# Attention and expert layer on one core: the order of every engine written out by a list scheduler inside the kernel

## The chip, the cores and the metric

The kernel runs on one core of one Trainium2 chip. The metric is the device time of one execution in microseconds. Three runs of the kernel before gave 1379.43, 1379.49 and 1369.95 us; the median is 1379.43 us. Besides those there is one profiled execution, from which every duration here is taken.

## The reference

Two stages follow each other: block-causal attention over 8 batches of 8 heads (576 positions, head size 64), and a two-layer network with a gate over the 4608 resulting tokens.

```python
scores = scale * np.matmul(q, k.transpose(0, 1, 3, 2))
scores = np.where(mask, scores, -1000000000.0)       # block_i >= block_j, blocks of 64
scores = scores - np.max(scores, axis=-1, keepdims=True)
attn = np.exp(scores)
attn = attn / (np.sum(attn, axis=-1, keepdims=True) + 1e-09)
attn_out = np.matmul(attn, v)
x = attn_out.transpose(0, 2, 1, 3).reshape(B * S, H * D)      # 4608 x 512
h = x @ w_in                                                  # 512 -> 2048
sp = np.maximum(h, 0.0) + np.log1p(np.exp(-np.abs(h)))
out = (h * erf(sp)) @ w_out                                   # 2048 -> 512
```

Products are made from two parts, a rounded high part and a low part that holds the rest, so each product of the network is three matmuls (high by high, high by low, low by high). The weights come as 64-bit numbers and are cut into those parts on the core.

## The kernel before, in words

**Attention.** The heads are numbered 0 to 63, eight to a batch. Per head, `load_qk` brings k and q (one transfer of SP's queue into the staging tile st, one of POOL's queue into one of four tiles qk, two more on SP's queue that copy inside SBUF), and POOL subtracts to make the low parts (L320, L321). `maxes` computes scores on TensorE (L332, tile s) and row maxima on VectorE (L335, tile mx); the maxima are transposed (L362), copied by ScalarE (L364) and put into the qk tile by a transfer issued from ScalarE's queue (L365). `probs` recomputes the scores transposed (L378, L379, tile t), ScalarE takes the exponentials (L383) into the tile p and rounds them (L389, ph), VectorE makes the low part (L390, pl). `pv` multiplies pairs of heads with v (L422) and with ones (L445), `scale_v` (L278) and `prep_v` (L299, L300) cut v for four heads at a time from a staging tile v that has one buffer, and `normalise` divides (L461 to L479) and stores x to DRAM as x_d (L480). A group of 256 tokens of x exists when the batch that holds its last token has gone through `normalise`, so x becomes available once in eight heads.

**The network, first part.** Of the 16 blocks of 128 hidden columns the first six are done on groups of 256 tokens: 18 groups by three units of two blocks are the 54 first-part units. A unit has 24 matmuls of 256 columns (up, L154), a gate (`gate`: ScalarE L123 once and L128 four times, VectorE L130 and L135, ScalarE L136, POOL L137) and 12 matmuls of 512 columns (down, L164); three units are followed by a store of the partial sums (L209, L210). **Second part.** The other ten blocks run on nine groups of 512 tokens, one block to a unit: 90 units of 12 up and 12 down matmuls of 512 columns. The ten weights of the second part are cut by five VectorE operations per half (L98, L99, L102, L104, L105), besides ScalarE (L101, L106) and POOL (L107, L108); so are the six of the first part, early in the attention.

**What sets the order.** Steps are Python closures. For every head `merge` interleaves the lists of steps; `moe1` is called once per head (RATE = 1) and hands out one step of a first-part unit, six steps per head after the last head (RATE2 = 6). The order in which the program is written, moved by `tc.cur_priority` for some kinds (`late`, PRIO), is the priority with which the framework's scheduler then orders every engine's queue. Each engine runs its queue in order.

**PSUM** has four pools: ps_o and ps_h with two banks each, ps_a with four during attention, and ps_o2 and ps_h2 with three and one after it.

Of the kernel before, what the change touches and what calls it, by code (L numbers as in the profile page):

```python
# [32 lines left out]

@with_exitstack
def tile_attention_moe(ctx: ExitStack, tc: tile.TileContext, qk, v, w, maskrows, sels, out):
# [8 lines left out]
    SP = 640  # L44
# [8 lines left out]
    SH = 384  # L53
    p0, p1, pars, fin = PAR

# [3 lines left out]
    wpool = ctx.enter_context(tc.tile_pool(name="wpool", bufs=F1))  # L59
    xpool = ctx.enter_context(tc.tile_pool(name="xpool", bufs=2))  # L60
    mpool = ctx.enter_context(tc.tile_pool(name="mpool", bufs=3))
    ps_o = ctx.enter_context(tc.tile_pool(name="ps_o", bufs=2, space=PSUM))
    ps_h = ctx.enter_context(tc.tile_pool(name="ps_h", bufs=2, space=PSUM))
# [21 lines left out]

    def room(pool, f):
        return [pool.tile([P, 2, DM], F32R, tag=t, name=f"{t}{f}") for t in ("whi", "wlo")]

    def load_weight(whi, wlo, stage, f):

        for s in range(2):
            nm = f"{f}_{s}"
            raw = stage[0][0].tile([P, stage[0][2]], I32, tag=stage[0][1][s], bufs=stage[0][3], name=f"raw{nm}")[:, : 2 * DM].rearrange("p (n t) -> p n t", t=2)
            nc.sync.dma_start(raw.rearrange("p n t -> p (n t)"), w[f, s].bitcast(I32))
            top, low = raw[:, :, 1], raw[:, :, 0]

            bits = stage[1][0].tile([P, stage[1][2]], I32, tag=stage[1][1], bufs=stage[1][3], name=f"bits{nm}")[:, :DM]
            nc.vector.tensor_scalar(out=bits, in0=top, scalar1=3, scalar2=0x3FFFFFF8, op0=ALU.logical_shift_left, op1=ALU.bitwise_and)  # L98
            nc.vector.scalar_tensor_tensor(out=bits, in0=top, scalar=-0x40000000, in1=bits, op0=ALU.bitwise_and, op1=ALU.bitwise_or)  # L99
            sq = stage[2][0].tile([P, stage[2][2]], F32, tag=stage[2][1], bufs=stage[2][3], name=f"sq{nm}")[:, :DM]  # L100
            nc.scalar.activation(sq, f32(top), AF.Square)  # L101
            nc.vector.scalar_tensor_tensor(out=sq, in0=sq, scalar=LEAST * LEAST, in1=f32(bits), op0=ALU.is_ge, op1=ALU.mult)  # L102

            nc.vector.tensor_scalar(out=bits, in0=sq.bitcast(I32), scalar1=-0x800000, scalar2=None, op0=ALU.bitwise_and)  # L104
            nc.vector.scalar_tensor_tensor(out=f32(bits), in0=low.bitcast(U32), scalar=2.0**-52, in1=f32(bits), op0=ALU.mult, op1=ALU.mult)  # L105
            nc.scalar.copy(whi[:, s, :], sq)  # L106
            nc.gpsimd.tensor_tensor(out=sq, in0=sq, in1=f32(whi[:, s, :]), op=ALU.subtract)  # L107
            nc.gpsimd.tensor_tensor(out=wlo[:, s, :], in0=sq, in1=f32(bits), op=ALU.add)  # L108
        return whi, wlo

    gpools = [mpool]

    def gate(h, name, gpool):

        n = h.shape[1]
        last = {}
        for k, o in enumerate(PROG):
            for i in o[1:]:
                last[i] = k
        gh, gl = (gpool.tile([P, n], F32R, tag=t, name=f"{name}_{t}") for t in ("gh", "gl"))  # L120
        regs = [mpool.tile([P, n], F32, tag="r0", name=f"{name}_r0")]
        free = [f32(gl), mpool.tile([P, n], F32, tag="r1", name=f"{name}_r1")]
        nc.scalar.activation(regs[0], h, AF.Tanh, bias=const(p1), scale=p0)  # L123
        for k, (o, pp) in enumerate(zip(PROG, pars)):
            free += [regs[i] for i in sorted(set(o[1:])) if last[i] == k]
            r = free.pop()
            if o[0] == "S":
                nc.scalar.activation(r, regs[o[1]], AF.Square, bias=const(pp[1]), scale=pp[0])  # L128
            elif o[0] == "M":
                nc.vector.scalar_tensor_tensor(out=r, in0=regs[o[1]], scalar=pp[0], in1=regs[o[2]], op0=ALU.add, op1=ALU.mult)  # L130
            else:
                nc.vector.scalar_tensor_tensor(out=r, in0=regs[o[1]], scalar=pp[0], in1=regs[o[2]], op0=ALU.mult, op1=ALU.add)
            regs.append(r)
        g = regs[-1]
        nc.vector.scalar_tensor_tensor(out=g, in0=g, scalar=fin, in1=h, op0=ALU.add, op1=ALU.mult)  # L135
        nc.scalar.copy(gh, g)  # L136
        nc.gpsimd.tensor_tensor(out=gl, in0=g, in1=f32(gh), op=ALU.subtract)  # L137
        return gh, gl

    hpools = [ps_h]  # L140
    turns = []

    def moe_unit(ws, xh, xl, o, tw, nu, u, name, first, last, spread):

        turns.append(u)
        h = hpools[len(turns) % len(hpools)].tile([P, nu, tw], F32, tag="h", name=f"{name}_h")
        parts = []

        def up(k, cs):
            whi, wlo = ws[u * nu + k]  # L150
            for cc in cs:
                sl = slice(cc * P, (cc + 1) * P)
# [25 lines left out]
    def merge(*lists):  # L178
        for step in merged(*lists):
            step()  # L180
# [36 lines left out]
    def moe1(ready, lag):  # L217
# [18 lines left out]
        if todo:  # L236
            todo.pop(0)()
# [429 lines left out]
```

## Time and profile before

| | |
|---|---|
| median of three runs | 1379.43 us |
| the profiled execution's own time | 1378.77 us |
| its span, first to last instruction | 1377.0 us |
| TensorE / ScalarE / VectorE / POOL busy | 93% / 71% / 57% / 44% |
| mean granted TensorE clock | 0.960 |

A row of the groups view names the line, engine and operation, the tile written and the tiles read, the shape and the count; then the busy time and the mean duration of one, and the engine's idle time just before these instructions with what ended it. A row of the stretches view gives, for a piece of the span, its length, then busy time and number of instructions of TensorE, its weight loads, VectorE, ScalarE and POOL, then the granted clock, the share of the transfer engines and their rate. Issuing a transfer is not counted as busy time of the engine that issues it. A matmul's row lasts longer than the distance to the next one, because matmuls overlap; TensorE's busy share therefore says that matmuls were in flight, not that they came at the highest rate.

### The profile page before, as it was taken

To read this page: it belongs to the slowest core of one execution; us is meant where nothing else is said; L and a number is where in the kernel's file an instruction comes from. 1 tells how busy PE (TensorE), PEld (TensorE's weight loads), DVE (VectorE), ACT (ScalarE), POOL (GpSimd) and SP (SyncE) were. 2 spreads that over 40 slices of the span, in tenths; PEclk is the share of its full clock that TensorE was granted. 3 is DMA by queue.
4 is the path that set the end of the run, shared out by engine and by line. 5 is a ranking of instruction groups with operands and counts; after the bars stand their busy time and mean duration, and the time that the engine had idled before them with its cause. 6 is when DMAs were issued, how large, how long until landed. Compare 5 with 4: busy or idle time off the path is not lost. (4 is left out here: it accounts for less than half of the span.)

```text
span 1377.0 us, 22100 instructions
## 1 busy us (share of the span) xinstructions
PE 1277.7 (93%) x8198; PEld 1021.0 (74%) x8198; DVE 782.0 (57%) x1237; ACT 971.7 (71%) x1781; POOL 599.3 (44%) x456
## 2 busy tenths in 40 slices
PE   2798999999999989989989998699999999999998
PEld 1455677777777768767778886578888888888887
DVE  5798977777777767767772227953233233232332
ACT  1466677678877858767777777577777777777775
POOL 3776765554655545654562225652222222222221
PEclk9898799999999989999899998899999999999999
DMA  9466757766777657675237224212113112211110
GB/s 235 123 188 162 200 147 191 190 171 190 199 180 206 172 133 195 144 196 162 104 127 245 92 92 154 77 49 74 62 61 123 61 61 85 100 62 61 62 62 31
DMA packets 89372, 179.97 MB, mean 131 GB/s; under 512 B 8540, under 2 KB 27292, under 8 KB 89264
## 3 DMA queue, kind: packets, MB, share of 16 engines
q1 hardware_dynamic: 79280, 159.41, 38.8%
q0 software_dynamic: 9344, 18.97, 6.2%
q8 instruction: 65, 1.06, 0.3%
q14 instruction: 43, 0.35, 0.1%
q10 hardware_dynamic: 640, 0.17, 0.1%
HBM read 112.29 MB, written 37.75 MB: 109 GB/s over the span
## 5 line engine op out<-in xcount | busy, mean ns | idle before, releaser
L128 ACT ACTIVATE m_r<-m_r,c 128x512 f32<-128x512 f32 x576 | 414.8, 722 | 113.4 <-DVE m_r L130 98.5
L137 POOL TENSOR_TENSOR m_gl<-m_r,m_gh 128x512 fp32r<-128x512 f32 x144 | 198.0, 1375 | 474.7 <-ACT m_gh L136 420.1
L130 DVE SCALAR_TENSOR_TENSOR m_r<-m_r,m_r 128x512 f32<-128x512 f32 x144 | 111.7, 776 | 331.2 <-ACT m_r L128 326.2
L154 PE MATMUL m_h<-xh,whi 128*128 128x256 f32 (+1 forms) x648 | 213.2, 329 | 11.6 <-DVE m_r L135 11.4
L154 PE MATMUL m_h<-xl,whi 128*128 128x256 f32 (+1 forms) x648 | 211.4, 326 | 0.0
L154 PE MATMUL m_h<-xh,wlo 128*128 128x256 f32 (+1 forms) x648 | 210.5, 325 | 0.0
L383 ACT ACTIVATE p<-t 128x288 f32<-128x288 f32 (+4 forms) x384 | 141.5, 387 | 96.7 <-PE t L379 58.8
L335 DVE TENSOR_REDUCE mx<-s 64x1 f32<-64x288 f32 (+4 forms) x384 | 170.2, 468 | 67.2 <-PE s L332 64.7
L164 PE MATMUL o<-whi,m_gh 128*128 128x512 f32 x432 | 174.0, 403 | 6.9 <-ACT ob L209 4.6
L164 PE MATMUL o<-wlo,m_gh 128*128 128x512 f32 x432 | 174.7, 404 | 0.0
L390 DVE TENSOR_TENSOR pl<-p,ph 128x832 f16<-128x832 f32 (+1 forms) x128 | 161.4, 1262 | 21.3 <-ACT ph L389 20.7
L332 PE MATMUL s<-qk 68*64 68x288 f32 (+3 forms) x384 | 132.2, 364 | 25.0 <-DVE mx L335 17.1
L164 PE MATMUL o<-whi,m_gl 128*128 128x512 f32 x432 | 152.4, 403 | 1.5 <-POOL m_gl L137 1.5
L378 PE MATMUL t<-qk 69*128 69x288 f32 (+4 forms) x384 | 134.7, 352 | 18.5 <-DMA qk<-mt 9.9
L154 PEld LDWEIGHTS m_h<-xh,whi 128*128 128x128 f32 x648 | 125.4, 193 | 34.3 <-DVE m_r L135 19.5
L320 POOL TENSOR_TENSOR qk<-st,qk 64x576 fp32r<-64x576 f32 x64 | 99.2, 1550 | 105.2 <-PE t L379 27.2
L321 POOL TENSOR_TENSOR qk<-st,qk 64x576 fp32r<-64x576 f32 x64 | 113.6, 1776 | 70.6 <-DMA qk<-qk 68.0
L135 DVE SCALAR_TENSOR_TENSOR m_r<-m_r,m_h 128x512 f32<-128x512 f32 x144 | 98.4, 683 | 79.1 <-ACT m_r L128 79.1
L154 PEld LDWEIGHTS m_h<-xl,whi 128*128 128x128 f32 x648 | 125.5, 194 | 15.2 <-issue 0.2
L154 PEld LDWEIGHTS m_h<-xh,wlo 128*128 128x128 f32 x648 | 125.4, 194 | 10.9 <-issue 1.3
L136 ACT CAST m_gh<-m_r 128x512 fp32r<-128x512 f32 x144 | 89.2, 619 | 51.6 <-DVE m_r L135 50.5
L379 PE MATMUL t<-qk 128*128 128x288 f32 (+4 forms) x384 | 123.9, 324 | 0.0
(83 smaller groups left out, 2367.0 us busy)
## 6 DMA issues: line engine op xcount, KB each, us to landing
st<-qk SPq DMA_DIRECT2D x64, 288.0 KB
qk<-qk POOLq DMA_DIRECT2D x64, 288.0 KB, 4.6
qk<-qk SPq DMA_DIRECT2D x64, 288.0 KB
x_d<-xs SPq DMA_DIRECT2D x32, 576.0 KB
raw<-w SPq DMA_DIRECT2D x32, 512.0 KB
v<-v SPq DMA_DIRECT2D x16, 640.0 KB
qk<-qk SPq DMA_DIRECT2D x64, 144.0 KB
xh<-x_d SPq DMA_DIRECT2D x18, 512.0 KB
```

The lines of the kernel that those rows point to most:

```text
L128: nc.scalar.activation(r, regs[o[1]], AF.Square, bias=const(pp[1]), scale=pp[0])
L130: nc.vector.scalar_tensor_tensor(out=r, in0=regs[o[1]], scalar=pp[0], in1=regs[o[2]], op0=ALU.add, op1=ALU.mult)
L137: nc.gpsimd.tensor_tensor(out=gl, in0=g, in1=f32(gh), op=ALU.subtract)
L154: nc.tensor.matmul(h[:, k, :], lhsT=a[:, 0, sl], rhs=x[:, cc, :], start=cc == 0 and i == 0, stop=cc == NCC - 1 and i == 2)
L164: nc.tensor.matmul(o[c], lhsT=a[:, sl], rhs=b_[:, 1, :], start=first and k == 0 and not lo and b_ is whi, stop=last and k == nu - 1 and lo)
L321: nc.gpsimd.tensor_tensor(out=t[D:, 1, :], in0=st[D:, :], in1=f32(t[D:, 1, :]), op=ALU.subtract)
L332: nc.tensor.matmul(dst[:r, :w_], lhsT=qh[:K, i * P : i * P + r], rhs=kh[:K, k0 : k0 + w_], start=True, stop=True)
L335: nc.vector.tensor_reduce(out=mx[:r, col : col + 1], in_=src, axis=AX.X, op=ALU.max, negate=True)
L378: nc.tensor.matmul(s[:kk, :w_], lhsT=kh[:K, ks], rhs=qh[:K, q0 : q0 + w_], start=True, stop=False)
L379: nc.tensor.matmul(s[:kk, :w_], lhsT=klh[:, ks], rhs=qhl[:, q0 : q0 + w_], start=False, stop=True)
L383: nc.scalar.activation(p32s[part][:kk, c : c + w_ - skip], s[:kk, skip:w_], AF.Exp, scale=SCALE)
L390: nc.vector.tensor_tensor(out=pl, in0=p, in1=ph, op=ALU.subtract)
```

## The change

The same operations with the same operands are no longer emitted as they are written. Each is recorded as a task with an engine, a duration in ns, a delay after it, the tiles it reads and writes and a priority (`plan.add`); `Plan.order` then runs a list schedule over all of them, and they are traced in the order of the start times that it found, under `tc.manual_schedule()`, so that this order is every engine's queue. Tile buffers are claimed in the plan too: a task that first uses a tile can't start before the plan has a free buffer.

The priority is the number of the head at which a step is written, plus its place within that head. `pv` steps are moved ahead by 0.7 (PV), the operations of a gate by 3 (GATE). The 49 units that need no later pools have the priority max(n + 1, 10 + 1.19 x index) where n is the head at which their x is known; a lower number goes first, and a ready task of any number goes when nothing ahead of it is ready. The pools of the second part (ps_o2, ps_h2, gpool, wpool2, bpool) open when all tasks of the attention era have run in the plan (`over`). Warm-up matmuls are 80 instead of 110. `sums` is one task instead of being cut by the merge.

```diff
+    HOP = 200.0
+    SPARE = 500.0
+    SWITCH = 90.0
...
+    def add(self, eng, ns, fn, r=(), w=(), lag=0.0, mode="f", off=0.0):
+        t = Task(len(self.tasks), eng, ns, lag, fn, self.prio + off, mode, self.era)
...
+                for o in t.outs:
+                    hop = 0.0 if o.eng == t.eng and not t.lag else self.HOP + (self.SPARE if o.eng == "PE" else 0.0)
+                    o.ready = max(o.ready, now + hop)
...
+            while pending and pending[0][0] <= now:
+                _, _, t = heapq.heappop(pending)
+                insort(ready.setdefault(t.eng, []), (t.prio, t.seq, t))
...
+        return sorted(self.tasks, key=lambda t: (t.at, t.seq))
...
+    GATE = -3.0
...
+                add("ACT", 722, lambda r=r, a=a, pp=pp: nc.scalar.activation(r[0](), a[0](), AF.Square, bias=const(pp[1]), scale=pp[0]), r=[a[1]], w=[r[1]])
...
+            add("ACT", 60, lambda: nc.scalar.dma_start(f32(qks[n % NB][D + 4 : D + 5, 3 * S :]).rearrange("o (i p) -> o i p", p=P), f32(mt())),
+                r=[mt], w=Q(n, "m"), lag=2500.0)
...
+        while units1 and units1[0][0] in known and len(units1) > TAIL:
+            at = max(n + BEHIND, 9 + BEHIND + (NT // T * NU - len(units1)) * spread)
+            if at > n + 8 and n < N + 3:
+                break
+            unit1(at, False)
...
+    over = Task(len(plan.tasks), "X", 0, 0.0, None, 0.0, "f", 0)
+    over.deps = {t for t in plan.tasks if t.era == 1}
...
+    with tc.manual_schedule():
+        for t in plan.order():
+            if not opened and any(b.late for b in t.bufs):
+                opened = True
+                era.close()
...
+            if t.fn:
+                t.fn()
```

**VectorE, from its first instruction.** Before (vm, vs, vsb belong to v; bits, sq and raw to the first weight; a number after an underscore is head, batch or weight):

```order
L278 TENSOR_REDUCE vm0_0_153<-v32_0_0_151 128x1
L526 CAST id16_209<-ident_77 128x128
L98 TENSOR_SCALAR bits0_0_329<-raw0_0_327 128x512
L283 TENSOR_REDUCE vs0_0_157<-vt0_0_155 1x1
L99 SCALAR_TENSOR_TENSOR bits0_0_329<-raw0_0_327,bits0_0_329 128x512
L284 TENSOR_SCALAR vs0_0_157<-vs0_0_157 1x1
L285 RECIPROCAL vs0_0_157<-vs0_0_157 1x1
L98 TENSOR_SCALAR bits0_1_342<-raw0_1_340 128x512
```

Now:

```order
L388 CAST id16_130<-ident_77 128x128
L471 TENSOR_REDUCE mx0_126<-s01_0_157 128x1 x2
L471 TENSOR_REDUCE mx0_126<-s2_0_162 128x1
L411 TENSOR_REDUCE vm0_0_185<-v32_0_0_141 128x1
L471 TENSOR_REDUCE mx0_126<-s4_0_0_164 64x1
L471 TENSOR_REDUCE mx0_126<-s4_0_1_167 64x1
L497 TENSOR_TENSOR mx0_126<-mx0_126 64x1
L471 TENSOR_REDUCE mx1_127<-s01_1_169 128x1 x2
```

The row maxima of head 0 stand first; before, 23 other operations (v and the first weights) stand ahead of them.

**ScalarE at head 21.** p32 is the tile p, t20 and t21 are the scores of heads 20 and 21, m1_1_2 is group 1, unit 2 of the first part. Before:

```order
L383 ACTIVATE p32_1_118<-t1_20_128_2885 128x448
L383 ACTIVATE p32_1_118<-t2_20_256_2927 128x320
L383 ACTIVATE p32_0_117<-t0_21_0_2943 128x288
L389 CAST ph1_20_2931<-p32_1_118 128x768
L136 CAST m1_1_1_gh_6900<-m1_1_1_r1_6903 128x512
L123 ACTIVATE m1_1_2_r0_8122<-m1_1_2_h_7162,c1_88 128x512
L425 ACTIVATE usb9_2822<-u4_1_1_2947,vsb2_0_2247 128x320
L383 ACTIVATE p32_0_117<-t0_21_288_2959 128x288
L128 ACTIVATE m1_1_2_r0_8122<-m1_1_2_r0_8122,c2_90 128x512
```

Now:

```order
L304 ACTIVATE m1_3_0_r0_3339<-m1_3_0_h_3288,c1_88 128x512
L310 ACTIVATE m1_3_0_r0_3339<-m1_3_0_r0_3339,c2_90 128x512
L310 ACTIVATE m1_3_0_r1_3346<-m1_3_0_r0_3339,c3_92 128x512
L319 CAST m1_2_2_gh_3350<-m1_2_2_r1_3299 128x512
L310 ACTIVATE m1_3_0_r1_3346<-m1_3_0_r1_3346,c4_94 128x512
L527 ACTIVATE p32_1_118<-t1_20_128_3322 128x448
L527 ACTIVATE p32_1_118<-t2_20_256_3327 128x320
L535 CAST ph1_20_3375<-p32_1_118 128x768
L310 ACTIVATE m1_3_0_r1_3346<-m1_3_0_r1_3346,c5_96 128x512
L527 ACTIVATE p32_0_117<-t0_21_0_3341 128x288
```

Before, a gate's operations stand one at a time between those of the heads all through the attention; now gates stand in runs. TensorE's queue shows the same in numbers: before, first-part matmuls stand between the scores of every two heads from head 12 on, and 28 of the 54 units have begun when the scores of head 63 start; now six units (once nine) stand together at heads 12 to 16, 20 to 24, 28 to 31 and so on, none in between, and 45 have begun by then.

**TensorE at the end of the attention** (t63 are head 63's scores, u its product with v, o1_8_1 the output of group 8). Before:

```order
L378 MATMUL t3_63_320_8055<-qk3_101 128x256
L379 MATMUL t3_63_320_8055<-qk3_101 128x256
L164 MATMUL o1_8_1_9332<-whi3_738,m1_8_1_gl_9420 128x512
L378 MATMUL t4_63_320_8066<-qk3_101 64x256
L379 MATMUL t4_63_320_8066<-qk3_101 64x256
L378 MATMUL t1_63_128_8074<-qk3_101 128x448
```

Now:

```order
L520 MATMUL t3_63_320_10238<-qk3_110 128x256
L521 MATMUL t3_63_320_10238<-qk3_110 128x256
L520 MATMUL t4_63_320_10246<-qk3_110 64x256
L521 MATMUL t4_63_320_10246<-qk3_110 64x256
L520 MATMUL t1_63_128_10250<-qk3_110 128x448
L521 MATMUL t1_63_128_10250<-qk3_110 128x448
```

Group 8 of 18 was being worked on; now groups up to 14 are finished, and the next first-part matmul after these rows is that of group 15, whose x holds tokens of the last batch, after 158 other rows. Nine units are left instead of 26. In the second part the down matmuls of a unit stood five units behind its up matmuls; now one or two.

More of the change, by code (lines that the diff above doesn't have):

```diff
@@ L1 @@
+import heapq
+from bisect import insort
 from contextlib import ExitStack
@@ L92, in load_weight @@
             nm = f"{f}_{s}"
[L93 to L98, printed above, removed]
@@ L105, in load_weight @@
[L105 to L115, printed above, removed]
+            braw = buf(stage[0][0], [P, stage[0][2]], I32, stage[0][1][s], f"raw{nm}", stage[0][3])
```

1008 lines of the change are left out of this document (588 added, 420 removed).

## The prediction

> **What bounds the kernel now.** I read the page first. It looks bound by TensorE, and I do not believe it for the whole span:
>
> ```profile
> PE 1277.7 (93%) x8198; PEld 1021.0 (74%) x8198; DVE 782.0 (57%) x1237; ACT 971.7 (71%) x1781; POOL 599.3 (44%) x456
> ```
>
> So next the stretches view, in four pieces: up to head 12, heads 12 to 63, the rest of the first part, the second part (times of TensorE, weight loads, VectorE, ScalarE, POOL), and below it five pieces of 50 us.
>
> ```profile
> 0.00:169.00 169.00, 124.86 (x850) 80.70 (x850) 135.70 (x222) 83.05 (x179) 107.42 (x98) 0.90 0.68 181
> 169.00:683.00 514.00, 486.41 (x4131) 386.44 (x4130) 378.05 (x655) 383.13 (x829) 280.97 (x205) 0.95 0.65 173
> 683.00:885.00 202.00, 185.41 (x1112) 156.56 (x1112) 106.64 (x133) 148.43 (x240) 82.84 (x57) 0.96 0.40 137
> 885.00:1377.00 492.00, 481.07 (x2111) 397.32 (x2109) 161.65 (x230) 357.06 (x535) 128.10 (x97) 0.99 0.20 67
> ...
> 50.00:100.00 50.00, 46.87 (x336) 29.10 (x334) 43.86 (x72) 30.51 (x69) 32.59 (x25) 0.96 0.67 176
> 100.00:150.00 50.00, 44.42 (x332) 28.89 (x331) 41.75 (x76) 29.49 (x68) 35.42 (x23) 0.79 0.61 170
> 300.00:350.00 50.00, 48.24 (x431) 38.35 (x431) 39.30 (x74) 40.85 (x91) 27.39 (x23) 1.00 0.69 192
> 850.00:900.00 50.00, 36.71 (x120) 27.67 (x121) 49.59 (x54) 31.18 (x53) 32.61 (x22) 0.80 0.32 106
> 1000.00:1050.00 50.00, 50.00 (x222) 41.44 (x221) 15.39 (x23) 37.02 (x55) 11.64 (x9) 1.00 0.26 85
> ```
>
> The second part is bound by TensorE: 222 matmuls of 512 columns in 50 us are 0.225 us each, and 90 units of 24 are 486.5 of its 492 us. No order shortens that. Heads 12 to 63 are different. At 0.225/512 = 0.44 ns a column a head has 5696 columns of scores (2.5 us), half a pair's 4800 columns against v (the two heads of a pair start together, 0.13 to 0.14 us for 320 columns in the rows below: 1.0 us) and, I estimate from what is left, 0.8 us of sums and transposes, 4.3 us in all. 26 units of 5.5 us come to that, 51 x 4.3 + 143 = 362 of 514 us: "busy" says 486 because each row outlasts the distance to the next.
>
> ```profile
> 481.51 0.30 PE L422 MATMUL u<-ph,vl 128*64 128x320 f16 x2
> 481.65 0.30 PE L422 MATMUL u<-pl,vh 128*64 128x320 f16 x2
> 481.78 0.30 PE L422 MATMUL u<-ph,vh 128*64 128x320 f16 x2
> ```
>
> What fills the heads is ScalarE, of whose time issuing the maxima's transfer (0.70 us a head) isn't in the busy column: 383.1 + 50 x 0.70 = 418 of 514 us, 81%, and 44.4 of 50 (89%) in the best piece. VectorE has 74%. Neither is full; they wait for each other in order. One such stall, of VectorE and then ScalarE:
>
> ```profile
> L365 ACTq DMA_DIRECT2D qk<-mt x64: 693/700/1264, 38.5 to 675.0; - x64
> ...
> 483.74 1.49 DVE L278 TENSOR_REDUCE vm<-v 128x1 f32<-128x1280 f32 x1 [5.47 <-DMA v<-v]
> ...
> 487.28 0.41 ACT L383 ACTIVATE p<-t 128x288 f32<-128x288 f32 x1 [6.40 <-DVE pl L390]
> ...
> DVE vm L278 <- DMA v<-v: 29.4, 8, 10.0
> ```
>
> A reduction of v stood at the head of VectorE's queue before its data had landed; pl behind it waited, and ScalarE waited for pl. Eight such waits are 29 us.
>
> **The change part by part.** It removes 30 warm-up matmuls, which only fill time in which TensorE waits for the first data, and adds nothing; the rest is order. I cost the warm-ups, the sums in one piece and the claims on PSUM at nothing (were the warm-ups in the way, 30 x 0.22 = 7 us). The transfers stay the same in number; a head's own (288 + 288 + 288 + 144 + 160 + 288 KB by the page) come to 1.46 MB, 200 GB/s at 7.25 us a head, and at 0.65 busy for 173 GB/s the transfer engines carry that at three quarters, so SP's queue is not the next to be late. *(a) Start.* The scores of head 0 are there at 14.8, their maxima begin at 27.8 because v and weights stand ahead on VectorE:
>
> ```profile
> 14.84 1.99 PE L332 MATMUL s<-qk 68*128 68x256 f32 x6
> ...
> 27.77 4.72 DVE L335 TENSOR_REDUCE mx<-s 128x1 f32<-128x128 f32 x12
> ```
>
> Now the maxima stand first. But VectorE must still cut six weights and serve twelve heads before head 12, and 135.7 of 169 us are already work: of the 33 us idle some 10 precede the first data. I take 10 us (0 to 20).
>
> *(b) Heads 12 to 63.* What a unit costs ScalarE and VectorE comes from these groups of the same 514 us:
>
> ```profile
> L128 ACT ACTIVATE m_r<-m_r,c 128x512 f32<-128x512 f32 x105 | 75.5, 720 | 2.3 <-DVE m_r L130 2.2
> L123 ACT ACTIVATE m_r<-m_h,c 128x512 f32<-128x512 f32 x26 | 17.8, 685 | 0.0
> L136 ACT CAST m_gh<-m_r 128x512 fp32r<-128x512 f32 x26 | 16.1, 619 | 0.9 <-DVE m_r L135 0.8
> L209 ACT COPY ob<-o 128x512 f32<-128x512 f32 x16 | 9.3, 579 | 1.0 <-PE o L164 1.0
> ...
> L130 DVE SCALAR_TENSOR_TENSOR m_r<-m_r,m_r 128x512 f32<-128x512 f32 x27 | 23.0, 851 | 0.3 <-ACT m_r L128 0.3
> L135 DVE SCALAR_TENSOR_TENSOR m_r<-m_r,m_h 128x512 f32<-128x512 f32 x26 | 17.5, 672 | 0.5 <-ACT m_r L128 0.5
> ```
>
> ScalarE (75.5 + 17.8 + 16.1 + 9.3)/26 = 4.56 us, VectorE 1.56 us. Without the units (118.7 and 40.5 us) and the few weight operations at the end of the stretch (about 5 and 12 us) a head costs ScalarE (418 - 118.7 - 5)/51 = 5.8 us and VectorE (378 - 40.5 - 12)/51 = 6.4 us. Now 45 units lie in this stretch, about 6.75 to every eight heads, and they lie together. I cost a period of eight heads in two pieces. The burst: four heads with 6.75 units, TensorE 4 x 4.3 + 6.75 x 5.5 = 54 us, ScalarE 4 x 5.8 + 6.75 x 4.56 = 54 us; at the 89% that ScalarE reaches in its best piece, 60.5 us. Four heads alone: VectorE bounds, 6.4 us at the 88% that it had from 50 to 100 us (43.86 of 50), 7.25 us, together 29 us. Period 89.5 us against 8 x 514/51 = 80.6 us now; 6.4 periods are 573 us, 59 more than 514. Bounds: ScalarE's whole work is 8 x 5.8 + 6.75 x 4.56 = 77 us, so 80 us is the least; the burst one after the other with the heads (the last rival) is 110 us. I stand nearer the lower end since 89% and 88% are rows of engines working beside each other, as they must here. The planned durations are near the rows (722 ns for L128, 720 here); the worst, the maxima's transfer at 60 ns against 700, is inside my 5.8 us, but the plan doesn't see it, which is why I don't go below 89%.
>
> *(c) After the last head.* Before, 26 units take 683 to about 886, which is 1377 - 486.5 and some 4 us for the end. Now nine are left, 9 x 5.5 = 50 us, but all nine need the last batch, and nothing covers it: from the last scores to the last store of x,
>
> ```profile
> L378 PE MATMUL t<-qk x384: 278/332/802, 40.4 to 683.4; 69*128 69x288 f32 x63, 69*128 69x256 f32 x63, 69*128 69x448 f32 x63, 69*128 69x320 f32 x2
> ...
> L480 SPq DMA_DIRECT2D x_d<-xs x32: 359/377/383, 101.3 to 699.3; - x32
> ...
> L187 SPq DMA_DIRECT2D xh<-x_d x27: 359/386/1165, 148.6 to 1250.3; - x27
> ...
> L154 PE MATMUL m_h<-xh,whi x648: 274/283/793, 155.9 to 1358.1; 128*128 128x256 f32 x108, 128*128 128x512 f32 x54
> ```
>
> 16 us, then the store (I estimate 5 us, from POOL's 4.6 us landings on the page) and from the first load to the first matmul 7 us: 28 us in which TensorE has only the end of the attention. Its cover, units of earlier groups, is gone. So 203 us become 78.
>
> *(d) The ten weights.* One costs VectorE twice the sum of these means, 8.5 us:
>
> ```profile
> L99 DVE SCALAR_TENSOR_TENSOR bits<-raw,bits 128x512 int32<-128x512 int32 x32 | 34.0, 1062 | 0.4
> L102 DVE SCALAR_TENSOR_TENSOR sq<-sq,bits 128x512 f32<-128x512 f32 x32 | 29.6, 925 | 1.7 <-ACT sq L101 0.6 <-DVE bits L99 0.5
> L105 DVE SCALAR_TENSOR_TENSOR bits<-raw,bits 128x512 f32<-128x512 uint32 x32 | 29.0, 907 | 0.4
> L98 DVE TENSOR_SCALAR bits<-raw 128x512 int32<-128x512 int32 x32 | 26.0, 812 | 7.9 <-POOL wlo L108 5.0 <-DMA raw<-w 2.9
> L104 DVE TENSOR_SCALAR bits<-sq 128x512 int32<-128x512 int32 x32 | 17.6, 550 | 0.3
> ```
>
> They stopped TensorE before: 13 us at 850 to 900, with VectorE at 49.59 of 50. Now 85 us of weights and 19 gates of 1.5 us stand in 78 us and the 54 us of the first group, 114 of 132: VectorE just suffices, and I charge 8 us (0 to 20).
>
> *(e) Second part.* Down matmuls follow their gate more closely. In the trace a gate takes from 1000.51 (first operation) to 1008.85 (its low part done):
>
> ```profile
> 1000.51 0.67 ACT L123 ACTIVATE m_r<-m_h,c 128x512 f32<-128x512 f32 x1
> ...
> 1006.81 0.62 ACT L136 CAST m_gh<-m_r 128x512 fp32r<-128x512 f32 x1 [0.30 <-DVE m_r L135]
> ...
> 1007.56 1.29 POOL L137 TENSOR_TENSOR m_gl<-m_r,m_gh 128x512 fp32r<-128x512 f32 x1 [4.13 <-ACT m_gh L136]
> ```
>
> 8.3 us, or 6.9 for the high part that goes first. In the new queue three groups of twelve and a bit stand between, 39 matmuls of 0.225 us, 8.8 us. It fits barely; I charge 7 us for 90 units (0 to 45, half a us each, were the gates late).
>
> *Sum*, in the profiled execution's own time (1378.8 us with 1.8 us around the span; the median is 1379.4): 683 - 10 + 59 + 78 + 8 + 491 + 7 + 2 = **1318 us**, 61 us less.
>
> **The rivals.** *The period shrinks to 80 us* because waits like v's all go: VectorE reached 99% at 850 to 900. Against it, there it worked on weights alone. 6.4 x 9.5 = 61 us less, and (e) at nothing: 1250 us.
>
> *The clock falls in the heads without units.* At 100 to 150 us, where the heads run alone, the row has clock 0.79 and 332 matmuls, at 300 to 350 clock 1.00 and 431. Heads alone then cost TensorE 8.6 us at half the clock instead of 7.25 us: 1.35 x 4 x 6.4 = 35 us more, 1353 us. For it speaks the row; against it that TensorE would then be full and the clock rises again. [...]
>
> *The gain is eaten*: ScalarE keeps its 81% (period 77/0.81 = 95 us) and the gates of (e) are late by a third of a us each, 30 us instead of 7: 1318 + 6.4 x 5.5 + 23 = 1376 us, no change.
>
> *Slower: bursts run instead of heads.* Gates have their priority moved ahead by 3, so on ScalarE they go before the exponentials of the heads; each unit's matmuls then take 5.5 us while heads stand, 6.75 x 5.5/0.9 = 41 us, and eight heads alone cost 8.6 us each (6.4 us at the 74% that VectorE has now, since p has one buffer and makes the two wait as in the 6.40 us row): 41 + 69 = 110 us. That is 1318 + 6.4 x 20.5 = 1449 us. It decides from a period of 99 us on. For it speaks the order with four gate operations in a row; against it that exponentials of the running heads stand between them.
>
> **How the numbers follow.** Chances: my sum 0.48, the short period 0.14, the clock 0.10, eaten 0.13, slower 0.15. A measurement here tells from no change what differs by about 1%, 14 us (1365.6 to 1393.2). The first three lie below 1366 but for a part of their spread: faster 0.70; within 1% 0.15; slower 0.15. The range goes from the short period, 1250, up to the eaten gain and a little of the slow case, 1390.
>
> **What would show it.** Right: the last scores at about 732 us, first-part matmuls in seven bursts, ScalarE in the stretch from head 12 at 85 to 90% with issues, a TensorE gap of 20 to 30 us behind the last head, the second part in 492 to 500 us. The waits of vm for v mostly gone. Wrong in (b): last scores beyond 790 us, heads standing still during bursts. Wrong in (c): the gap over 40 us. Wrong in (e): TensorE under 95% after the first group, released by gates. If the end of attention comes before 690 us, I took the shares of ScalarE and VectorE too low.

## The result, and the profile after

The changed kernel takes 1526.61 us (median of four runs, 1524.83 to 1530.26) against 1379.46 us for the kernel before on the same chip: ratio 1.1096, 95% interval 1.1035 to 1.1156. It is 147 us slower; the forecast was 61 us faster. The profiled execution took 1524.83 us, its span 1522.9 us. The page, then the stretches view in the four pieces of the prediction (up to head 12, heads 12 to 63, the rest of the first part, the second part), cut where they now end; a head is placed by the start of its 448-column score matmul:

```profile
PE 1365.3 (90%) x8168; PEld 1083.9 (71%) x8168; DVE 791.7 (52%) x1237; ACT 984.4 (65%) x1781; POOL 580.0 (38%) x456
```
```profile
0.00:203.00 203.00, 143.06 (x931) 97.36 (x932) 143.95 (x227) 92.47 (x190) 112.48 (x102) 0.74 0.61 156
203.00:900.00 697.00, 654.65 (x4655) 517.89 (x4653) 390.54 (x684) 472.56 (x940) 283.77 (x219) 0.83 0.50 137
900.00:1034.00 134.00, 94.14 (x526) 79.03 (x524) 89.73 (x104) 80.31 (x134) 61.01 (x42) 0.83 0.42 148
1034.00:1523.00 489.00, 473.41 (x2064) 389.67 (x2062) 167.50 (x224) 339.02 (x518) 122.74 (x94) 0.99 0.20 67
```

The second row holds the loss: 697 us where before had 514. It holds 42 units now instead of 26 (by their up matmuls), yet VectorE does nearly the same work in it (390.5 against 378.1 us), and ScalarE's busy share falls from 75% to 68%: the stretch is not fuller, it waits. The third row is 134 us instead of 202, and 86 was forecast. The second part has hardly changed (489 us, before 492).

Where TensorE's up matmuls of the network lie, in 40 equal slices of the span, first before, then after (lines: up is L330 after the change, down L349, scores L520 and L521, scores for the maxima L467, exponentials L527, a gate's ScalarE L304 and L310, its VectorE L314 and L318, maxima L471, a weight's first VectorE operation L277):

```profile
busy tenths in 40 slices 0000656577665637656499999999999999999996
```
```profile
busy tenths in 40 slices 0000690890970990980940929977999999999997
```

Before, every slice has some of them from the fifth on; after, they come in blocks with empty slices between, as the order had shown. TensorE inside one block, from the timeline:

```profile
396.60 0.44 PE L521 MATMUL t<-qk 128*128 128x288 f32 x1
396.84 0.41 PE L330 MATMUL m_h<-xh,whi 128*128 128x256 f32 x1
...
404.53 0.28 PE L330 MATMUL m_h<-xh,wlo 128*128 128x256 f32 x1
404.74 0.30 PE L569 MATMUL u<-ph,vh 128*64 128x256 f16 x2
...
420.38 0.28 PE L330 MATMUL m_h<-xh,wlo 128*128 128x256 f32 x1
420.50 0.28 PE L520 MATMUL t<-qk 69*128 69x256 f32 x1
```

Between the scores at 396.60 and the next at 420.50 lie 24 us: 48 ups (two units), products with v and sums, one score tile for the maxima, twelve ups, the 24 downs of two units, 36 more ups. TensorE is dense (busy 23.5 of the 24 us), but the running head gets none of its scores t, and the engines behind it stand still, as the waits of ScalarE and VectorE in the same 24 us say, and the waits view of the whole span, after and then before:

```profile
401.98 0.69 ACT L304 ACTIVATE m_r<-m_h,c 128x512 f32<-128x512 f32 x1 [4.46 <-PE m_h L330]
...
420.94 0.69 DVE L314 SCALAR_TENSOR_TENSOR m_r<-m_r,m_r 128x512 f32<-128x512 f32 x1 [10.29 <-ACT m_r L310]
```
```profile
DVE m_r L314 <- ACT m_r L310: 269.9, 106, 11.3
DVE mx L471 <- PE s L467: 171.6, 117, 14.3
...
ACT m_r L304 <- PE m_h L330: 128.1, 84, 7.5
```
```profile
DVE m_r L130 <- ACT m_r L128: 326.2, 106, 4.0
DVE mx L335 <- PE s L332: 64.7, 102, 2.1
...
ACT m_r L123 <- PE m_h L154: 3.7, 5, 1.9
```

The columns are us in total, number of waits, the longest. VectorE's wait inside the gates was larger in total before, so it is not the loss. What has grown are the waits for TensorE: VectorE waits 171.6 us for score tiles to take maxima from instead of 64.7, ScalarE 128.1 us for a unit's ups instead of 3.7.

### The profile page after: what moved, and what is told of

Its sections match the earlier page's. It is cut to its first block, busy times and chain, and to the rows that moved or that the text cites. A ratio compares the mean times of both kernels' runs of the same rounds, so it can differ in the third digit from the quotient of the medians.

```text
span 1522.9 us, 21901 instructions
## 1 busy us (share of the span) xinstructions
PE 1365.3 (90%) x8168; PEld 1083.9 (71%) x8168; DVE 791.7 (52%) x1237; ACT 984.4 (65%) x1781; POOL 580.0 (38%) x456
## 4 chain that ended last, share of the span: by engine, by line
PE 51%; ACT 8%; DVE 6%; DMA 3%; issue 2%; SPq 1%; POOL 0%; DVEq 0%; ACTq 0%; POOLq 0%
PE o L349 20%; PE m_h L330 20%; ACT m_r L310 3%; PE u L569 3%; PE s L467 2%; PE t L520 2%; PE t L521 1%; DMA qk<-mt 1%; ACT p L527 1%; DMA raw<-w 1%; PE us L594 1%; PE rt L612 1%; PE rb L630 1%; DVE m_r L314 1%; ACT m_r L304 1%
## 5 line engine op out<-in xcount | busy, mean ns | idle before, releaser
L310 ACT ACTIVATE m_r<-m_r,c 128x512 f32<-128x512 f32 x576 | 406.6, 720 | 72.3 <-DVE m_r L314 56.1
L314 DVE SCALAR_TENSOR_TENSOR m_r<-m_r,m_r 128x512 f32<-128x512 f32 x144 | 126.0, 875 | 286.9 <-ACT m_r L310 269.9
L471 DVE TENSOR_REDUCE mx<-s 64x1 f32<-64x288 f32 (+4 forms) x384 | 170.3, 468 | 173.1 <-PE s L467 171.6
L330 PE MATMUL m_h<-xh,whi 128*128 128x256 f32 (+1 forms) x648 | 218.6, 337 | 35.5 <-DVE m_r L318 25.2
L527 ACT ACTIVATE p<-t 128x288 f32<-128x288 f32 (+4 forms) x384 | 140.7, 387 | 131.2 <-PE t L521 107.5
L330 PE MATMUL m_h<-xl,whi 128*128 128x256 f32 (+1 forms) x648 | 215.4, 332 | 2.0 <-DMA xl<-x_d 2.0
L330 PE MATMUL m_h<-xh,wlo 128*128 128x256 f32 (+1 forms) x648 | 215.0, 332 | 0.0
L520 PE MATMUL t<-qk 69*128 69x288 f32 (+4 forms) x384 | 153.7, 401 | 38.7 <-DVE mx L471 18.4
L349 PE MATMUL o<-whi,m_gh 128*128 128x512 f32 x432 | 176.6, 409 | 10.7 <-ACT m_gh L319 10.6
L304 ACT ACTIVATE m_r<-m_h,c 128x512 f32<-128x512 f32 x144 | 98.6, 684 | 129.1 <-PE m_h L330 128.1
L467 PE MATMUL s<-qk 68*128 68x256 f32 (+3 forms) x384 | 145.5, 417 | 33.9 <-DMA qk<-qk 21.1
L349 PE MATMUL o<-wlo,m_gh 128*128 128x512 f32 x432 | 172.7, 400 | 0.0
L330 PEld LDWEIGHTS m_h<-xh,whi 128*128 128x128 f32 x648 | 132.3, 204 | 50.4 <-DVE m_r L318 27.2
L536 DVE TENSOR_TENSOR pl<-p,ph 128x832 f16<-128x832 f32 (+1 forms) x128 | 147.2, 1153 | 15.4 <-ACT ph L535 14.8
L318 DVE SCALAR_TENSOR_TENSOR m_r<-m_r,m_h 128x512 f32<-128x512 f32 x144 | 98.5, 684 | 106.6 <-ACT m_r L310 106.3
L455 POOL TENSOR_TENSOR qk<-st,qk 64x576 fp32r<-64x576 f32 x64 | 102.5, 1602 | 112.2 <-PE t L521 30.1
L330 PEld LDWEIGHTS m_h<-xl,whi 128*128 128x128 f32 x648 | 132.2, 204 | 11.9 <-DMA xl<-x_d 2.3
L330 PEld LDWEIGHTS m_h<-xh,wlo 128*128 128x128 f32 x648 | 131.8, 203 | 8.8
L521 PE MATMUL t<-qk 128*128 128x288 f32 (+4 forms) x384 | 137.2, 359 | 0.0
L520 PEld LDWEIGHTS t<-qk 69*128 69x128 f32 (+1 forms) x384 | 83.5, 217 | 73.4 <-DVE mx L471 26.6
L456 POOL TENSOR_TENSOR qk<-st,qk 64x576 fp32r<-64x576 f32 x64 | 101.2, 1582 | 68.9 <-DMA qk<-qk 66.3
```

The costliest lines, as they stand in the source:

```text
L304: add("ACT", 690, lambda: nc.scalar.activation(br[0](), h(), AF.Tanh, bias=const(p1), scale=p0), r=kh, w=[br[0]])
L310: add("ACT", 722, lambda r=r, a=a, pp=pp: nc.scalar.activation(r[0](), a[0](), AF.Square, bias=const(pp[1]), scale=pp[0]), r=[a[1]], w=[r[1]])
L314: add("DVE", 890, lambda r=r, a=a, c=c, pp=pp, ops=ops: nc.vector.scalar_tensor_tensor(out=r[0](), in0=a[0](), scalar=pp[0], in1=c[0](), o ...
L330: nc.tensor.matmul(bh()[:, k, :], lhsT=a(0)[:, cc * P : (cc + 1) * P], rhs=x()[:, cc, :], start=cc == 0 and i == 0, stop=cc == NCC - 1 and ...
L349: nc.tensor.matmul(o[c](), lhsT=a()[:, sl], rhs=b_(1), start=first and k == 0 and not lo and b_ is whi, stop=last and k == nu - 1 and lo)
L467: add("PE", mmns(w_), lambda: nc.tensor.matmul(s()[:r, c0 : c0 + w_], lhsT=qh[:K, i * P : i * P + r], rhs=kh[:K, k0 : k0 + w_], start=True ...
```

## The experiments

All runs are of the whole computation. Unless an interval is given a time is one run, beside a run of the kernel before at 1377 to 1381 us. Ten runs of one of these kernels lie between 1375.76 and 1386.06 us, so single runs less than about 1% apart tell no difference. "The stretch" is that from head 12 to head 63; units are counted by their up matmuls.

**Units spread over the heads, still ahead of them.**

```diff
+    for at, ups in held.items():          # ups: the unit's up matmuls
+        if int(at) + 3 < N:
+            for t in ups:
+                t.deps.add(anchor[int(at) + 3])   # scores of the third head after its number
```

> The changed kernel, but in the plan the first matmuls of a first-part unit may not start before the scores of the third head after its priority number, so that units stand one to a head and not six together (42 instead of 45 begun by the last head). Theory A, the heads that stand alone let the TensorE clock fall to half and are then bound by TensorE: clock above 0.92 from head 12 to 63 (0.83 in the changed kernel), that stretch 560 to 610 us instead of 697, time 1400 to 1450. Theory B, the planned order itself stalls the engines because its durations and waits are not those of the chip: stretch within 30 us of 697, time 1490 to 1550.

Measured: 1556.96 us, worse than the changed kernel.

```profile
185.00:925.00 740.00, 656.30 (x4694) 520.08 (x4690) 397.35 (x688) 465.25 (x938) 275.46 (x221) 0.85 0.47 130
```

Neither theory has its numbers. The clock rose to 0.85 only, so this run can't judge theory A, and the stretch is 43 us longer, where B allowed 30. What it shows is that spacing the units does not help as long as each one, once it starts, goes ahead of the heads.

**The clock.** One more 512-column matmul ahead of each score tile, in the heads without units:

```diff
             def go():
+                if n < 12 or n % 8 < 4:
+                    nc.tensor.matmul(s(), lhsT=ident16, rhs=..., start=True, stop=True)
                 nc.tensor.matmul(s()[:kk, :w_], lhsT=kh[:K, ks], ...
```

> The changed kernel in its own order, with one more matmul of 512 columns, whose result is overwritten, ahead of each score tile of the heads up to 11 and of the first four of every later eight: 6 x 0.22 us a head of added TensorE work, some 50 us in all. Theory A: the clock in the stretches without units goes from 0.61 to 0.75 up to 0.9 or more, four heads alone take about 32 instead of 40 us, time 1440 to 1480 in spite of the added work. Theory B: clock or not, the heads keep their pace or get slower by the added work, time 1520 to 1580.

Measured: 1512.71 us.

```profile
202.00:886.00 684.00, 628.61 (x4799) 492.43 (x4797) 391.36 (x684) 472.71 (x941) 280.61 (x219) 0.94 0.51 140
```

The clock is back at 0.94 and the stretch is 13 us shorter. Four heads alone went from 40.6 to 37.1 us (means over the six such groups), the four with units from 68.4 to 69.7. Theory A has its clock and not its time: raising the clock gains 14 us of 147, hardly more than single runs can tell. That is a net figure, with the filler's own work in it; the clock's whole price was not measured.

**Heads alone under the order of before.** The units of the kernel before handed out only after the last head, without and with ten warm-up matmuls a head:

```diff
-            if not xs1:
+            if n < 11:                            # warm-ups; n < N in the second run
...
-            lists.append((late("moe", [lambda: moe1(ready, LAG)] * k), 0, 1))
+            lists.append((late("moe", [lambda: moe1(ready if n >= N else 0, LAG)] * k), 0, 1))
```

> The kernel before with its scheduler, but no first-part unit before the last head (all 54 after it), so that heads 12 to 63 stand alone under the old order. Theory A: the clock falls there too, mean below 0.75, and a head takes 9.5 us or more although ScalarE and VectorE have less to do than with units (10.1 us a head with 26 units). Theory B: clock above 0.9 and 7 to 8 us a head, since nothing but the list schedule is at fault.

> The same as the one before with ten warm-up matmuls of 512 columns at every head and not only the first eleven, 2.2 us of TensorE work more per head that nothing needs. Theory A: clock 0.9 or more, and the heads get faster by 1 us or more each (about 8 to 8.5 us) with more work. Theory B: heads slower or the same as without the fillers.

Measured: 1389.79 and 1485.72 us. The first is no test: the framework's scheduler put 27.7 units back into the stretch (before has 26.1). In the second 3.8 are left there, and the heads take 473.5/51 = 9.3 us each at clock 0.96, with the filler and the 3.8 units in them. The 7.25 us of the prediction is not reached there either, but the run doesn't say what the heads alone would take.

**Units behind the heads: one number.**

```diff
-            unit1(at, False)
+            unit1(at + 200, False)
```

> One number changed: the 49 units that need no later pools get their priority plus 200, so that every head's step goes ahead of every unit and a unit only takes what the heads leave free. Theory C (the unit's number is lower than the number of the head that runs when its x arrives, about 3 heads late, and gates another 3 lower, so whole units go ahead of the heads' scores on TensorE and ScalarE and are done in series with the heads): units spread over the heads, the stretch from head 12 to head 63 falls from 697 to 520-570 us, the granted clock in it rises from 0.83 to over 0.93, and the time is 1360-1420. Rival D (the units are ready only in bursts because x is finished once in eight heads, and a list order can't spread them whatever their number): the stretch stays at 660-700 and the time at 1490-1530. Rival E (the heads' own chain is what is slow in this order, with or without units): the stretch 600-660, 1440-1490.

Measured: 1409.42 us, 117 us less than the changed kernel.

```profile
191.00:719.00 528.00, 508.48 (x4372) 412.95 (x4371) 379.38 (x660) 425.30 (x880) 274.37 (x207) 0.97 0.62 172
```
```profile
busy tenths in 40 slices 0000086896779869659489999569999999999997
```
```profile
398.49 0.28 PE L330 MATMUL m_h<-xh,wlo 128*128 128x256 f32 x1
398.61 0.37 PE L520 MATMUL t<-qk 69*128 69x448 f32 x1
...
399.17 0.31 PE L521 MATMUL t<-qk 128*128 128x320 f32 x1
399.32 0.28 PE L330 MATMUL m_h<-xh,whi 128*128 128x256 f32 x1
```

The stretch is 528 us, ScalarE is at 81%, the clock at 0.97. The empty slices between the blocks are gone, and on TensorE two tiles of scores stand between two groups of ups. Over the whole span VectorE's wait for score tiles falls from 171.6 to 99.1 us, ScalarE's for a unit's ups from 128.1 to 75.0. Theory C is shown: nothing but the units' numbers was changed, and with numbers above those of the heads the list order spreads the units by itself. Rivals D and E fall. The clock's recovery (0.83 to 0.97) is part of the 117 us.

**The gates' number.**

```diff
-    GATE = -3.0
+    GATE = 0.0
```

> The changed kernel with the gates at their unit's own number instead of 3 lower; the units' own numbers stay. My losing case in the prediction blamed this shift for the bursts. If it is what puts units ahead of heads: the stretch from head 12 to head 63 falls by over 60 us from 697 and the time below 1465. Theory C (the unit's own number is lower than that of the head that runs, gates or not): stretch 670-710 us, bursts stay, 1505-1545.

Measured: 1534.53 us, the stretch 690 us, as theory C had it. That the gates were moved ahead is not the cause.

**Units recorded after the heads.**

```diff
-        while units1 and units1[0][0] in known and len(units1) > TAIL:
+        while n >= N + 3 and units1 and units1[0][0] in known and len(units1) > TAIL:
```

> The units are recorded after all heads instead of between them, so their numbers are all above those of the heads, and the buffers that heads and units share are claimed by the heads first. Under theory C this does the same for the heads as the number plus 200: the stretch from head 12 to head 63 520-570 us, the time 1340-1420; against the other kernel it tells whether the place in the record matters as well as the number (C: within 2%). Rivals D and E: as there, 1440-1530.

Measured: 1386.91 us, 1.6% below the kernel with the number alone, within the 2% of theory C. The stretch holds 38.5 units in 549 us (35.0 in 529 there), and the last head is followed by the second part's first unit after 102 us instead of 143.

**What a head costs without units.** Recorded after the heads, held until head 63's last scores, the clock kept up (0.97 and 0.95 in the rows) by the extra matmul in every head; then the same with all eight PSUM banks for the heads:

```diff
+    for t in held:
+        t.deps.add(anchor[N - 1])
...
-        k = len(turn) % 8 if slot < 8 else 0     # only in the second of the two
+        k = len(turn) % 8
```

> Every first-part unit waits for the last scores of head 63, so the heads run alone; a 512-column matmul ahead of each score tile keeps the clock up (1.3 us of TensorE a head). All work is done, in another order. This measures a head without units in the new order: the prediction had 7.25 us (VectorE at 88%). Theory P (four PSUM banks set the pace of heads alone): 9.0-9.6 us a head, stretch 460-490 us, VectorE at 65-75% in it; the prediction's own: 7.0-7.6 us, 360-390. After the last head all 54 units and the weights: time 1430-1500.

> As the kernel before it, and the heads may use all eight PSUM banks (every second, third and fifth of eight tiles in the banks that the units would use) through the whole attention instead of up to head 8 alone. Theory P (the banks set the pace): 7.0-7.9 us a head, stretch 355-405 us, VectorE over 80% in it, time 80-110 us shorter than the kernel with four. Rival (the one buffer of each half of p, or the maxima's way through ScalarE and a transfer, sets it; or the clock): 8.7-9.6 us a head, no difference over 2%.

Measured: 1478.22 and 1460.24 us; their stretches:

```profile
192.00:630.00 438.00, 403.95 (x3435) 269.46 (x3433) 321.11 (x591) 293.58 (x648) 213.19 (x174) 0.97 0.63 168
```
```profile
185.00:602.00 417.00, 387.64 (x3464) 274.52 (x3463) 331.19 (x589) 287.58 (x645) 222.36 (x171) 0.95 0.70 179
```

A head alone is 438/51 = 8.6 us, VectorE at 73%; with eight banks 8.2 us, at 79%. Neither the prediction's 7.0 to 7.6 us nor theory P's 9.0 to 9.6 was met with four banks, and with eight theory P expected 7.0 to 7.9: four banks cost 5%, not the 1.35 us between 8.6 and 7.25. What holds the heads back with eight banks stays open; the largest waits left there are ScalarE's for scores and POOL's for a free qk tile.

**The start.** All on the kernel with units recorded after the heads, whose head 12 is at 189.5 us (before: 168.7): more warm-ups; the first two weights ahead of the maxima again; the weights written at heads 2, 3, 5, 6, 8, 9 (with the second staging tile, below).

```diff
-    WARM = 10                       # rec_warm; and for n < 11 instead of 8
+    WARM = 25
...
+    plan.prio = -1.5                # rec_early
+    for _ in range(2):
+        next_w1()
...
-    W1 = [1, 2, 3, 4, 7, 8]         # late
+    W1 = [2, 3, 5, 6, 8, 9]
```

> The kernel with the units recorded after the heads (1386.9 us, head 12 at 189.5 us, clock 0.70 up to head 11) with 275 warm-up matmuls at the lowest priority among heads 0 to 10 instead of 80 among heads 0 to 7. If the low clock is what makes the first twelve heads 20 us later than before: clock over 0.9 there, head 12 at 165-175 us, time 1362-1375. If VectorE's work is what sets them (144 us of it up to head 12, little of it in the first 30 us): clock up, head 12 at 184-192, time 1380-1392.

> The same kernel (1386.9 us) with the first two weights of the first part ahead of head 0's row maxima on VectorE, as they stood before the change. If the step that puts the maxima first is what costs the start (VectorE's time in the first 50 us is lost and the weights come back later between heads): head 0 back at 45-50 us, head 12 at 170-180 instead of 189.5, time 1367-1380. If VectorE's place for the weights doesn't matter: head 12 at 186-194, 1383-1392.

> The kernel with the second staging tile (1376.3 us, head 12 at 187.5 us) with the six weights of the first part written at heads 2, 3, 5, 6, 8, 9 instead of 1, 2, 3, 4, 7, 8. If the start is long because weight operations stand in runs ahead of the heads' maxima on VectorE, which then stands idle once the weights are done (25 of 40 us from 160 on): head 12 at 172-182, time 1362-1372. If the sum of VectorE's work with its waits sets it whatever the order: head 12 at 185-191, 1372-1382.

Measured: head 12 at 188.3, 193.5 and 193.2 us; times 1379.86, 1388.17 and 1391.79 us. From 40 to 120 us, with 80 and with 275 warm-ups:

```profile
40.00:120.00 80.00, 54.58 (x382) 35.83 (x380) 70.10 (x108) 40.19 (x85) 52.08 (x36) 0.68 0.58 154
```
```profile
40.00:120.00 80.00, 77.20 (x565) 45.35 (x563) 70.99 (x108) 40.13 (x87) 52.65 (x35) 1.00 0.58 154
```

The clock goes from 0.68 to 1.00 there, and head 12 comes 1 us earlier. From 120 to 160 us it is 0.67 in that run too, so it clears the clock for the heads up to 7 alone (119 us against 120). The second run had head 0 later than expected (55 us) and head 12 where VectorE's place for the weights doesn't matter; the third missed both of its ranges. In two executions of the kernel with the second staging tile head 12 was at 187.5 and 194.1 us, so none of the three moved it by more than it moves by itself. None explains the late start; it stays open.

**The ten weights.** The second half of each early weight staged in the tile of xs; then all of this together, the first two of the six late weights staged in tiles of the second part's x and six weights instead of five asked for ahead of the second part besides:

```diff
-        load_weight(w2[-1], (("a", ("v32", "v32"), 4 * 5 * D, 1), ...
+        load_weight(w2[-1], (("a", ("v32", "xs"), 4 * 5 * D, 1), ...
...
-    AHEAD = 5                                                            # combo alone
+    AHEAD = 6
...
-            load_weight(w2[-1], (("x", ("xh", "xl"), 2 * DM, 2), ...        # combo alone
+            load_weight(w2[-1], (("b", ...) if len(w2) < 7 else ("x", ...), ...
```

> The same kernel (1386.9 us) with the second half of each of the four early weights of the second part staged in the tile of xs, not in the one buffer of v32. Theory T (the early weights go one after the other through one buffer, about 11 us a half, and the last of them opens the second part's pools): the four are done 20-40 us earlier (the first of the later six starts at 800-820 instead of 838), the first ten units of the second part take 70-80 us instead of 93, time 1360-1377. If the four weights that must wait for the first part's buffers decide it: 88-95 us, 1380-1390.

> Everything that a run has spoken for or left undecided: units recorded after the heads, second staging tile, weights written later, 275 warm-ups, and of the six late weights the first two staged in the tiles of the second part's x instead of the first part's, which the last groups still hold. If the late weights start too late because of that staging: the first of them under 815 us, the first ten units of the second part at 70-82 us, time 1345-1365. If VectorE's own work on them (about 5 us a half) sets it: 88-95 us, 1365-1380.

> The kernel with units recorded after the heads and the second staging tile again, timed against the kernel before. By its one run (1376.3) no difference: 1370-1388, ratio 0.995-1.006. Theory C in full, with the place of the units in the order as the main cause of the loss, holds if it stays over 130 us below the changed kernel.

Measured: 1376.3 us in the first run and 1380.43 us (median of ten) in the repeat, ratio to before 1.0006, interval 0.998 to 1.0032; all together 1378.42 us, ratio 0.9989, interval 0.9958 to 1.002. The early weights begin their last half at 786 instead of 810 us, the late ones start at 827 instead of 838 (817 with all together), and the second part's first ten units take 89 us instead of 93 (82 with all together). Theory T is right about the early weights, which end 24 us sooner, and wrong about what that brings: the late ones start 11 us sooner and the first ten units save 4. All together reach the 82 us and not the time that was expected with it. No version beats the kernel before; with the units' place mended the two orders are equal within 0.5%. Of the 146 us that came back, 117 came with the number (1526.61 to 1409.42), 22.5 with the place in the record (1386.91), and 6.5 with the staging tile (1380.43), the last too little for single runs to tell.

## Why the prediction was wrong, step by step

The forecast put the last scores at 732 us; they came at 900. The 207 us between 1318 and 1525 are 44 at the start, 124 in heads 12 to 63, 48 after the last head, and -9 in the second part.

**(b) Heads 12 to 63, wrong: both pieces of the period.** The six periods after head 15 have a mean of 109 us, where I had 89.5: the four heads with units 68.4 us (62.9 to 83.4) instead of 60.5, the four alone 40.6 us (35.5 to 42.9) instead of 29. Times 6.4 that is 51 + 74 = 125 for the 124 us missed. The burst failed at the step "at the 89% that ScalarE reaches in its best piece": that row came from units lying between the operations of heads. Here they were ahead of them, and 6.5 units added (68.4 - 4 x 8.6)/6.5 = 5.2 us each, nearly the 5.5 us of TensorE that a unit holds; put behind the heads, 35 units add (528.6 - 438.6)/35 = 2.6 us each. The four heads alone failed at "VectorE bounds, 6.4 us at the 88%": VectorE's 88% was that of a piece in which it cut weights too, and heads alone give it 73%, 8.6 us. The filler took 3.5 us off four of them (40.6 to 37.1), which is what the low clock (0.83 in the stretch, 0.94 with the filler) costs them, net of the filler's own work; of the 6.2 us above 4 x 8.6 = 34.4 the other 2.7 stay open. The sign that the prediction named for this, last scores beyond 790 us and heads standing still during bursts, is what came.

**The slower rival, right in size, wrong in cause.** It had 41 + 69 = 110 us a period, with eight heads at 8.6 us each; 109 and 8.6 were measured. That the sums agree is in part luck: the units added 34 us, not 41, and 6 us lie in the four heads alone, which took 40.6 us in that order. I blamed the gates' -3. With it undone the time does not fall; the unit's own number decides. I had the order before me, with its six units in a row and none between, and the argument against the rival ("exponentials of the running heads stand between them") looked at ScalarE's queue alone. On TensorE's queue there were no scores between the ups to make exponentials from.

**The clock rival, partly right:** 0.60 to 0.64 from 50 to 150 us, 0.83 in the stretch, 0.50 from 258 to 292 us (last row below); raising it again gained 14 us net, where the rival had 35.

**(a) Start, wrong in sign.** The maxima of head 0 do begin 12 us sooner (16.0 instead of 27.8 us, its 448-column scores at 34.6 instead of 49.5), and head 11 is 18 us later (174.8 against 156.6); the first block of units makes head 12 another 16 us late. The step that failed is that what head 0 wins, head 12 wins too. By head 4 it is gone (89 us, before 86). VectorE's place for the weights is not the reason by the second run of the start; up to head 11 VectorE is busy 133.4 of 174.8 us, before 123.7 of 156.6. Why it takes longer is the open point above.

**(c) The exposed chain, right.** 28 us were forecast between the last scores and the first matmul of the last batch, 22 measured:

```profile
922.53 0.58 PE L330 MATMUL m_h<-xh,whi 128*128 128x256 f32 x1 [10.27 <-DMA xh<-x_d]
```

The nine units behind it took 63 us instead of 50 (922 to 985).

**(d) The ten weights, mis-sized.** I spread 85 us of VectorE evenly over the 132 us after the last head. The first four weights begin before the last head and pass half by half through the one buffer of v; their loads are issued at

```profile
883.96 0.33 SPq L275 DMA_DIRECT2D raw<-w  x1
896.04 0.35 SPq L275 DMA_DIRECT2D raw<-w  x1
...
942.00 0.36 SPq L275 DMA_DIRECT2D raw<-w  x1
```

and the other six start only at 973.8: their pools open when the last of the first four is done (its last POOL operation ends at 953.9), and their first load is issued at 962.7. They and the gates hold VectorE at 69.25 of 86 us while the second part's first ten units take 86 us; their matmuls are 54 us, so 32 are lost where I charged 8. In 21.2 of them, six times, TensorE waits for the gate's operation L318, which stands among those of the weights on VectorE:

```profile
985.00:1071.00 86.00, 64.54 (x244) 50.01 (x242) 69.25 (x70) 51.99 (x84) 48.80 (x32) 0.88 0.19 64
```
```profile
PE m_h L330 <- DVE m_r L318: 21.2, 6, 6.5
```

Before, the same ten units took 62 us; the six weights began 28 us ahead of them there, under first-part units. The price of 8.5 us a weight was low as well: it is the mean over all 32 halves, and the twelve late ones cost VectorE 9.8 us a weight, before and after.

**(e) Second part, right with a smaller price.** The down matmuls find their gates done; TensorE has no hole:

```profile
1100.00:1150.00 50.00, 50.00 (x223) 41.40 (x222) 15.54 (x23) 35.69 (x54) 11.65 (x9) 1.00 0.25 85
```

From the eleventh unit to the end 451.5 us against 452.1 before; the 7 us charged were not needed. **The waits for v** were to be mostly gone: vm waits 22.7 us, six times, instead of 29.4, so most of them stayed. And the count was right: 45 units had begun by head 63, though 42 of them in the stretch, where the prediction put all 45. Doing more units under the heads was worth nothing, since they took the heads' place.

## What to carry to other kernels

A list scheduler obeys the number; filler work that has to wait for its input must carry a number behind everything that will be running when the input arrives, not behind what was running when the work was written down. When an order shows a block of filler with none of the main chain's instructions between, cost it as a sum, on the engine that feeds the chain, and cost the stretch without filler from a trace of that stretch alone, not from the best share of a fuller one.

## What the runs showed of the hardware

**VectorE's weight operation ends just after POOL's.** The same L277 with POOL idle, and with a POOL operation that started 0.4 us earlier (first VectorE, then POOL):

```profile
973.79 0.43 DVE L277 TENSOR_SCALAR bits<-raw 128x512 int32<-128x512 int32 x1 [9.51 <-DMA raw<-w]
...
1013.83 1.49 DVE L277 TENSOR_SCALAR bits<-raw 128x512 int32<-128x512 int32 x1
```
```profile
1013.44 1.60 POOL L291 TENSOR_TENSOR wlo<-sq,bits 128x512 fp32r<-128x512 f32 x1
```

It ends 0.3 us after POOL's does. Nine of the twelve late ones begin while POOL works, and all nine end 0.28 or 0.29 us after it; the other three take 0.41 to 0.43 us. The twelve have a mean of 1.18 us, against the 0.81 of the prediction's row; the same twelve had 1.09 before, so this is a part of the price in (d) and not of the change. One earlier operation, at 53.33, took 0.41 us beside a POOL subtraction (L456, 53.23 to 55.01), so not every one of POOL's makes L277 longer. Why the nine are longer isn't shown by these runs.

**The clock stays at half for 34 us with matmuls in flight.**

```profile
258.00:292.00 34.00, 33.28 (x170) 24.29 (x170) 21.37 (x41) 18.94 (x41) 15.15 (x12) 0.50 0.70 190
```

TensorE is busy 33.28 of these 34 us, so the argument against the clock rival, that with TensorE full the clock rises again, does not hold in this row. At 396.84 it is at half still (0.51 up to 401.66), the ups coming 0.21 us apart, and from 401.66, after 4.8 us of them, they come 0.12 us apart (1.00 up to 420.50). What brings the clock back isn't shown by these runs.
